# Spreading attention weights over key bands on 128 partitions instead of 80, with 64x32 matmul tiles and a new order of instructions

## The chip, the cores and the metric

The kernel runs on one core of a Trainium2 chip. A core has five engines that run at the same time, each with its own queue of instructions: PE (TensorE: matmuls and transposes against an identity), DVE (VectorE), ACT (ScalarE), POOL (GpSimd) and SP (SyncE, which here only issues DMAs). Engines wait for each other through semaphores. The metric is the time of one execution on the device in microseconds (us). Three executions of the kernel before took 189.2, 189.23 and 190.11 us, a median of 189.23. The profiled execution is a separate one, with a time of its own.

## The reference

The input is 2048 rows of 448 numbers. One attention layer and one MLP layer with a shift between rows follow each other, each behind a layernorm and with a residual:

```python
qkv = x @ wqkv                                # 16 heads of 28, S = 2048 rows
idx = pos[:, None] - 2 * arange(8)[None, :]   # 8 keys per query, every second row back
logits = einsum("bhsd,bhswd->bhsw", q, k[idx]) * 28 ** -0.5   # -1e9 where idx < 0
attn = softmax(logits)
A = einsum("bhsw,bhswd->bhsd", attn, v[idx]) @ wo

h  = gelu(layernorm(y) @ w1)
hs = concat(four quarters of h, shifted by +1, -1, +2, -2 rows) @ w2
x1 = y + hs
B  = x1 + gelu(layernorm(x1) @ w3) @ w4

y   = x + A(layernorm(x))
out = y + B(y)
```

w1 and w2 are 448 x 448, w3 is 448 x 1792 and w4 is 1792 x 448.

## The kernel before, in words

The rows are taken in four blocks of 512 (t = 0 to 3), each of four tiles of 128 rows. Per block the stages are N1 (layernorm, and the turning of its result so that the features lie on partitions), A1 (q and k), V (v), A2 (the logits: DVE multiplies q by shifted k, the products `qk_r`, and PE sums them over a head's features), S (softmax and the turning of its result), A3 (the weighted sum over v), O (w_o and the residual), B1 (layernorm) and M (w1 and gelu). The rest goes by five units of tiles (u = 0 to 4): B2 (w2 on shifted columns), T (layernorm), W3 (w3 and gelu) and B3 (w4, the residual and the store).

The change touches the way from the softmax to the weighted sum. A query needs eight keys that lie two rows apart. `phase_A2` ends with a multiplication that writes the normalised weights p into `pb`: for each of 8 groups of 64 queries, a row of 80 keys (16 of them, `PADK`, belong to the group before), of which each query fills its eight. PE turns `pb` against the identity in 64-row halves, so that keys lie on partitions, and copies put it into `pt[t]` (80 x 1024). `phase_A3` goes four times per block (`il`) over 128 queries. DVE multiplies a slice of `pt` with the 0/1 mask `bmask` (80 x 64), spread out so that every query has its own column: `bd_r` (80 x 2048). This is the group "bd_r<-arena,bmask" of the profile. PE then does 32 matmuls, with weights from `vw` (v, 80 keys by 32 columns for one head) and 64 moving columns of `bd_r`, on four column tiles of the array (j), into one PSUM bank, and one copy takes the bank to `actT`, the input of O. `vw` is v with its keys moved to the right partitions: `phase_V` copies v into `vt` (128 rows a tile) and issues DMAs from `vt` to `vw`: `a` (64 rows), `b` (80 rows) and `c` (the 16 rows of padding of three tiles) for each block, and `p` (the padding from the block before) from block 1 on.

Other transfers on SP are the loads of the inputs and weights, small copies within "arena" that give k its padding and its last 64 features their second half (the "kk" and "kr" pieces), the stores, and the DMA transposes `actT<-lntm`, which turn a normalised block where the table `TURN` says `d`.

The order of all instructions is written out by hand in the list `ORDER`: each number is one recorded operation (an instruction or a group of matmuls), and each engine gets its own operations in this order. `OTHER` lists the operations that go to their second engine: PSUM copies by default run on ACT and then on DVE, and the p multiplication by default on DVE and then on POOL. The tables `NORM`, `STATS` and `POWER` choose engines for the layernorms' parts. `arrange` (L191) adds the rule on transposes: a DMA transpose waits for all plain DMAs (stores aside) issued since the transpose before it, and all plain DMAs after it wait for it. All recorded instructions are issued by one line, L983, so that a line number tells nothing in this profile, and the names of the tiles and their shapes do.

PE, DVE, ACT and SP therefore each work through a fixed queue. An instruction whose input is late holds up all that stand behind it on its engine.

Of the kernel before, what the change touches and what calls it, by code (L numbers as in the profile page):

```python
# [6 lines left out]
ALU = mybir.AluOpType  # L7
# [10 lines left out]
RESIDUAL = 'ttvv'  # L18
ORDER = """
# [29 lines left out]
"""  # L49
OTHER = """  # L50
102 186 187 381 490 493 496 499 502 505 549
# [229 lines left out]
def bass_sequential_preLN__sliding_local_dilated__mixer_s_mlp__prompt_kernel(  # L281
# [9 lines left out]
    PADK = 16  # L291
    KW = 80
    KVW = PADK + 512
# [17 lines left out]
    with ExitStack() as es:  # L311
# [5 lines left out]
        bd_r = sb("bd_r", [KW, NBD, 2048], BF16)  # L317
        vt = sb("vt", [128, 2, 4, 512], BF16)
        vw = sb("vw", [KW, 2, 8, 512], BF16)
        bmask = sb("bmask", [KW, 64], BF16)  # L320
        lntm = sb("lntm", [128, NLN, 4, 512], BF16)
        actT = sb("actT", [128, NACT, 4, 4, 128], BF16)
        h3T = sb("h3T", [128, NF + 2, 512], BF16)
        wo_s = sb("wo_s", [128, 4, D], BF16)
# [92 lines left out]
        for z in (vt[:].rearrange("p s i (h n) -> p (s i h) n", n=32)[:, :, DH:32], pb[:], wo_s[:]):  # L417
            dve("memset", ap=z, constant=0.0)
# [606 lines left out]
```

## Time and profile before

| what | before |
| --- | --- |
| median of 3 runs (lowest, highest) | 189.23 us (189.2, 190.11) |
| profiled execution: its time, its span | 189.32 us, 187.5 us |
| PE busy, matmuls | 179.2 us (96% of the span), 2434 |
| DVE busy, instructions | 126.6 us (68%), 224 |
| ACT busy, instructions | 123.9 us (66%), 282 |
| POOL busy | 29.2 us (16%) |
| granted PE clock | 0.999 |
| DMA | 18.06 MB, 96 GB/s on average |

The span is the time from the first to the last recorded instruction, and the run's own time is 1.82 us longer than it. A busy share is an average over the whole span; the stretches differ much. In the slices, each digit is the busy share of one fortieth of the span in tenths. A group row reads: line, engine, operation, output and inputs with their shapes, count, then busy us in total and mean ns of one, then the idle time just before these instructions and what ended it. The mean length of one matmul or copy is longer than its pitch where instructions of one engine overlap. In a row of the chain of waits stand the start, the length and the work that the end depends on, in order of time. A row of a timeline gives the start, the length up to the last end, the instructions and their count.

### The profile page before, as it was taken

What the parts mean: (1) busy time and instruction counts of PE and PEld (TensorE: products, weight loads), DVE (VectorE), ACT (ScalarE), POOL (GpSimd) and SP (SyncE); (2) the same over time, 40 slices, a digit from 0 to 9 for tenths busy, and PEclk for the clock granted to TensorE, in tenths of its full rate; (3) what the DMA queues carried; (4) which work ended last, traced back from release to release, by engine and by line L of the source; (5) the groups of instructions that cost most, each with busy time, mean ns of one, the idle gap of its engine ahead of it and who ended that gap; (6) DMA issues with size and microseconds to landing.
All of it is one profiled execution on the core that took longest, in us unless ns stands there. A gap on an engine that the chain in (4) does not pass through costs nothing.

```text
span 187.5 us, 5641 instructions
## 1 busy us (share of the span) xinstructions
PE 179.2 (96%) x2434; PEld 102.4 (55%) x2434; DVE 126.6 (68%) x224; ACT 123.9 (66%) x282; POOL 29.2 (16%) x63
## 2 busy tenths in 40 slices
PE   6999999999988799999999999999999999999994
PEld 2694434355443345477445555555556665666882
DVE  7799999999999999997297278470057357000503
ACT  4679999989999897988976447505775004822340
POOL 4230000000004101004801200200002662500000
PEclk9999999999999999999999999999999999999999
DMA  5995724676644655453645000371000432400111
GB/s 133 359 286 100 105 59 101 112 177 128 144 129 75 155 144 139 121 154 104 117 126 98 3 0 3 68 149 36 0 0 3 89 96 77 105 3 0 66 36 49
DMA packets 36577, 18.06 MB, mean 96 GB/s; under 512 B 25304, under 2 KB 36040, under 8 KB 36552
## 3 DMA queue, kind: packets, MB, share of 16 engines
q1 hardware_dynamic: 36552, 17.70, 40.2%
q8 instruction: 19, 0.31, 0.7%
q14 instruction: 6, 0.05, 0.1%
HBM read 7.91 MB, written 1.84 MB: 52 GB/s over the span
## 4 chain that ended last, share of the span: by engine, by line
PE 78%; ACT 12%; DVE 4%; DMA 4%; issue 1%; SPq 0%
PE ps L983 78%; ACT arena L983 5%; ACT lntm L983 3%; DMA actT<-lntm 2%; ACT vt L983 2%; DVE st L983 1%; DMA xin<-in_A_x_dram 1%; ACT xin L983 1%; DVE lntm L983 1%; DVE bd_r L983 1%; DVE qk_r L983 1%; ACT rs_x L983 0%; DVE ls L983 0%; DVE mx L983 0%; DVE mv L983 0%
## 5 line engine op out<-in xcount | busy, mean ns | idle before, releaser
L983 PE MATMUL ps<-actT,arena 64*128 64x512 bf16 (+1 forms) x756 | 69.1, 329 | 0.4 <-ACT vt L983 0.4
L983 ACT ACTIVATE h3T<-ps 128x512 bf16<-128x512 f32 (+1 forms) x70 | 31.1, 515 | 40.8 <-PE ps L983 40.5
L983 PEld LDWEIGHTS ps<-actT,arena 64*128 64x128 bf16 x756 | 38.8, 94 | 24.9 <-PE ps L983 0.8
L983 PE MATMUL ps<-arena,h3T 64*128 64x448 bf16 (+2 forms) x434 | 43.7, 343 | 0.1
L983 ACT ACTIVATE arena<-ps 128x512 bf16<-128x512 f32 (+3 forms) x62 | 31.3, 544 | 7.0 <-PE ps L983 6.4
L983 PEld LDWEIGHTS ps<-arena,h3T 64*128 64x128 bf16 (+1 forms) x434 | 26.3, 94 | 16.1 <-PE ps L983 0.5
L983 DVE TENSOR_TENSOR qk_r<-arena 128x4096 bf16<-128x4096 bf16 (+1 forms) x16 | 32.0, 2014 | 0.0
L983 DVE SCALAR_TENSOR_TENSOR qk_r<-ps,mrs,arena 128x448 bf16<-128x448 f32 (+1 forms) x17 | 10.5, 652 | 30.9 <-PE ps L983 25.4
L983 POOL TENSOR_TENSOR arena<-arena,xin 128x448 f32<-128x448 f32 x16 | 16.1, 1037 | 19.8 <-DVE lntm L983 19.8
L983 DVE TENSOR_TENSOR bd_r<-arena,bmask 80x2048 bf16<-80x2048 bf16 x16 | 18.8, 1210 | 0.0
L983 DVE SCALAR_TENSOR_TENSOR arena<-xin,rs_y,ps 128x448 f32<-128x448 bf16 x16 | 10.2, 674 | 11.6 <-PE ps L983 9.6
L983 PE MATMUL ps<-wo_s,actT 64*128 64x448 bf16 x128 | 14.4, 350 | 1.0 <-ACT actT L983 0.7
L983 PE MATMUL ps<-w_s,arena 64*128 64x448 bf16 (+1 forms) x128 | 14.2, 350 | 0.4 <-ACT arena L983 0.3
L983 PE MATMUL ps<-actT,w_s 64*112 64x512 bf16 x112 | 13.4, 379 | 0.8 <-DMA actT<-lntm 0.6
L983 PE MATMUL ps<-arena,actT 64*128 64x448 bf16 x112 | 12.4, 350 | 0.1
L983 ACT ACTIVATE lntm<-xin,nm 128x448 bf16<-128x448 bf16 x16 | 10.5, 663 | 2.4 <-DVE nm L983 2.4
L983 POOL TENSOR_TENSOR pb<-ls,mx 128x512 bf16<-128x512 f32 x2 | 3.5, 1730 | 48.3 <-ACT mx L983 48.3
L983 ACT ACTIVATE actT<-ps 128x512 bf16<-128x512 f32 (+2 forms) x18 | 10.6, 645 | 0.0
L983 PEld LDWEIGHTS ps<-actT,w_s 64*112 64x112 bf16 x112 | 7.1, 127 | 6.3 <-PE ps L983 1.0
L983 PEld LDWEIGHTS ps<-wo_s,actT 64*128 64x128 bf16 x128 | 5.8, 94 | 7.6 <-ACT actT L983 1.9
L983 PEld LDWEIGHTS ps<-w_s,arena 64*128 64x128 bf16 (+1 forms) x128 | 6.4, 94 | 6.6 <-PE ps L983 1.0
L983 DVE BATCH_NORM_STATS2 st<-xin 128x6 f32<-128x448 bf16 x16 | 9.1, 614 | 0.9 <-DMA xin<-in_A_x_dram 0.9
(71 smaller groups left out, 160.9 us busy)
## 6 DMA issues: line engine op xcount, KB each, us to landing
arena<-in_B_w_dram SPq DMA_DIRECT2D x2, 896.0 KB, 5.5
out_dram<-qk_r SPq DMA_DIRECT2D x15, 112.0 KB, 1.8
arena<-in_B_w_dram SPq DMA_DIRECT2D x2, 784.0 KB, 5.0
vw<-vt SPq DMA_DIRECT2D x4, 320.0 KB, 3.2
vw<-vt SPq DMA_DIRECT2D x4, 256.0 KB, 4.7
arena<-in_A_wqkv_dram SPq DMA_DIRECT2D x2, 448.0 KB, 4.5
xin<-in_A_x_dram SPq DMA_DIRECT2D x2, 448.0 KB, 6.9
xin<-in_A_x_dram SPq DMA_DIRECT2D x3, 224.0 KB, 5.2
```

The source lines that it names most:

```text
L983: inst = getattr(eng, meth)(**kw)
```

## The change

The table `BAND` gives each block a form: blocks 0 to 2 take the new one ("h"), block 3 the old one ("w"). In the new form, bands of 32 queries by 48 keys stand on both halves of the partitions (rows 0 to 47 and 64 to 111). The p multiplication writes `pb_h` (128 columns a group instead of 80), PE turns 64x128 pieces of it, and `pt` has 128 rows. A3 goes twice over a pair of tiles (256 queries): one DVE multiplication of 128 x 2048 with a mask `bmask_h` (128 x 32), then two groups of 64 matmuls with 48x32 weights and 32 moving columns, on eight tiles of 64x32 (two row halves by four column tiles), into two banks, one for each half, and a copy for each bank. The matmuls of the kernel go from 2434 to 2818.

The DMAs that fill `vw` are cut otherwise in blocks 0 to 2: four pieces (32, 48, 48 and 48 rows) instead of two (64 and 80 rows), and `c` and `p` as before: two more DMAs a block. The setup has one more memset on DVE (`pb_h`), a memset and two mask selections on POOL and two reductions on DVE (`bmask_h`).

`ORDER` and `OTHER` are new throughout. Among other things, ACT has 10 table loads instead of 12 and two normalisations fewer, DVE has two normalisations more and two copies of 128x512 fewer (and one of 64x256 more); between the DMA transposes of blocks 2 and 3 stand ten plain DMAs instead of six, and between that of block 3 and the first of B1 18 instead of 16. `V_FIRST` is False and changes nothing.

```diff
...
 RESIDUAL = 'ttvv'
+BAND = 'hhhw'
+V_FIRST = False
 ORDER = """
-8 9 10 12 13 29 7 0 1 39 40 41 42 43 30 44 33 14 15 16 17 18 19 20 21 22 23 45 46 47 6 34 5 35 2 48 32 50 51 36 55 56
...
+9 10 11 8 5 13 14 15 16 17 18 19 20 21 22 23 0 1 3 4 45 46 47 6 48 49 50 30 31 39 40 2 7 56 51 52 53 54 41 57 61 62 58
...
 OTHER = """
-102 186 187 381 490 493 496 499 502 505 549
+192 193 195 282 355 389 496 499 505 511 555 556
...
+    QB, KB = 32, 48
...
-        bd_r = sb("bd_r", [KW, NBD, 2048], BF16)
+        bd_r = sb("bd_r", [128, NBD, 2048], BF16)
         vt = sb("vt", [128, 2, 4, 512], BF16)
-        vw = sb("vw", [KW, 2, 8, 512], BF16)
+        vw = sb("vw", [128, 2, 8, 512], BF16)
         bmask = sb("bmask", [KW, 64], BF16)
+        bmask_h = sb("bmask_h", [128, QB], BF16)
...
+        pb_h = sb("pb_h", [128, NSM, NW * 128], BF16)
...
-        pt = [arv(A_KV + t * KVB + 4 * KVW, KW, 1024) for t in range(NST)]
+        pt = [arv(A_KV + t * KVB + 4 * KVW, KW if BAND[t] == "w" else 128, 1024) for t in range(NST)]
...
-        for z in (vt[:].rearrange("p s i (h n) -> p (s i h) n", n=32)[:, :, DH:32], pb[:], wo_s[:]):
+        for z in (vt[:].rearrange("p s i (h n) -> p (s i h) n", n=32)[:, :, DH:32], pb[:], pb_h[:], wo_s[:]):
...
+            par = ls[:, 0, 168:192].bitcast(BF16).rearrange("p (e j) -> p e j", e=2)
+            pool("memset", ap=par, constant=0.0)
+            for base in (0, 64):
+                pool("affine_select", out=par, in_=par, pattern=[[1, 2], [2, KB // 2]], compare_op=ALU.not_equal, fill=1.0, base=base, channel_multiplier=-1)
+            for e in range(2):
+                dve("tensor_reduce", out=bmask_h[:].rearrange("p (m e r) -> p m e r", m=2, e=2)[:, :, e, :],
+                    in_=bass.AP(par.tensor, par.offset + e * (KB // 2) + 1, [list(par.ap[0]), [8, 2], [1, NW], [1, 8]]), axis=AX.X, op=ALU.max)
...
-            dma("vwa%d" % sl, vw[PADK:KW, sl, 0:8:2, :], vt[0:64, sl, :, :], 64 * 4096)
-            dma("vwb%d" % sl, vw[0:KW, sl, 1:8:2, :], vt[48:128, sl, :, :], 80 * 4096)
+            if BAND[t] == "w":
+                pieces = (("a", PADK, 0, 0, 64), ("b", 0, 1, 48, 128))
+            else:
+                pieces = (("a", PADK, 0, 0, QB), ("b", 64, 0, PADK, 64), ("d", 0, 1, 64 - PADK, 64 + QB), ("e", 64, 1, 64 + PADK, 128))
+            for name, to, odd, lo, hi in pieces:
+                dma("vw%s%d" % (name, sl), vw[to:to + hi - lo, sl, odd:8:2, :], vt[lo:hi, sl, :, :], (hi - lo) * 4096)
             dma("vwc%d" % sl, vw[0:PADK, sl, 2:8:2, :], vt[112:128, sl, 0:3, :], 16 * 3072)
...
             row = lambda v, off, step: bass.AP(v, off, [[v.shape[1] * v.shape[2], 128], [step, NW], [16, 4], [DIL, NW], [1, DIL]])
-            mult = dict(out=row(pb, sl * NW * KW + DIL, KW + DIL), in0=row(ls, sl * 512, 64),
-                        in1=bass.AP(zs, sl * 64, [[64 * NSM, 128], [8, NW], [2, 4], [0, NW], [1, DIL]]), op=ALU.mult)
+            by_half = lambda v, off, step, half: bass.AP(v, off, [[v.shape[1] * v.shape[2], 128], [step, NW], [half, 2], [16, 2], [DIL, NW], [1, DIL]])
+            whole = BAND[t] == "w"
+            if not whole:
+                mult = dict(out=by_half(pb_h, sl * NW * 128 + DIL, 128 + DIL, 64), in0=by_half(ls, sl * 512, 64, QB),
+                            in1=bass.AP(zs, sl * 64, [[64 * NSM, 128], [8, NW], [4, 2], [2, 2], [0, NW], [1, DIL]]), op=ALU.mult)
+            else:
+                mult = dict(out=row(pb, sl * NW * KW + DIL, KW + DIL), in0=row(ls, sl * 512, 64),
+                            in1=bass.AP(zs, sl * 64, [[64 * NSM, 128], [8, NW], [2, 4], [0, NW], [1, DIL]]), op=ALU.mult)
             S.add("dve", "tensor_tensor", alts=[("pool", [("tensor_tensor", mult)])], **mult)
             banks = [_Tile(P_bank), _Tile(P_bank)]
 
             def turn(h, r):
                 part = (TOP, BOT)[h]
-                return (h, dict(out=banks[h](lambda v: v[0:KW, 64 * r:64 * r + 64]), lhsT=pb[part, sl, r * KW:(r + 1) * KW], rhs=ident[part, part],
-                                start=True, stop=True), 64)
+                src = pb[part, sl, r * KW:(r + 1) * KW] if whole else pb_h[part, sl, r * 128:(r + 1) * 128]
+                return (h, dict(out=banks[h](lambda v: v[0:src.shape[1], 64 * r:64 * r + 64]), lhsT=src, rhs=ident[part, part], start=True, stop=True), 64)
 
             steps([turn(h, r) for r in range(NW) for h in range(2)])
             for h, b in enumerate(banks):
-                copy(pt[t].rearrange("p (n r) -> p n r", r=NW)[:, 64 * h:64 * h + 64, :], b(lambda v: v[0:KW, :].rearrange("p (r n) -> p n r", r=NW)))
+                copy(pt[t].rearrange("p (n r) -> p n r", r=NW)[:, 64 * h:64 * h + 64, :], b(lambda v: v[0:KW if whole else 128, :].rearrange("p (r n) -> p n r", r=NW)))
 
         def phase_A3(t):
             a = _Tile(P_act)
             sl = t % 2
-            for il in range(4):
+            for il in range(4 if BAND[t] == "w" else 0):
                 bd = _Tile(P_bd)
                 b = _Tile(P_bank)
-                dve("tensor_tensor", block=True, out=bd(lambda v: v.rearrange("p (n g r) -> p n g r", g=8, r=NW)),
+                dve("tensor_tensor", block=True, out=bd(lambda v: v[0:KW, :].rearrange("p (n g r) -> p n g r", g=8, r=NW)),
                     in0=pt[t][:, il * 256:il * 256 + 256].rearrange("p (n r) -> p n r", r=NW).unsqueeze(2).broadcast_to([KW, 32, 8, NW]),
                     in1=bmask[:].rearrange("p (g r) -> p g r", r=NW).unsqueeze(1).broadcast_to([KW, 32, 8, NW]), op=ALU.mult)
                 mms([(b(lambda v, j=j, lo=128 * c + 64 * a2: v[32 * j:32 * j + 32, lo:lo + 64]),
-                      vw[:, sl, 2 * il + a2, (4 * c + j) * 32:(4 * c + j) * 32 + 32],
-                      bd(lambda v, lo=(16 * a2 + 4 * c + j) * 64: v[:, lo:lo + 64]), True, True, 64, j)
+                      vw[0:KW, sl, 2 * il + a2, (4 * c + j) * 32:(4 * c + j) * 32 + 32],
+                      bd(lambda v, lo=(16 * a2 + 4 * c + j) * 64: v[0:KW, lo:lo + 64]), True, True, 64, j)
                      for c in range(4) for a2 in range(2) for j in range(4)])
                 copy(a(lambda v, il=il: v[:, il, :, :].rearrange("p c n -> p (c n)").rearrange("p (m r e) -> p m r e", r=NW, e=2)),
                      b(lambda v: v.rearrange("p (m e r) -> p m r e", r=NW, e=2)))
+            for pair in range(2 if BAND[t] == "h" else 0):
+                bd = _Tile(P_bd)
+                banks = [_Tile(P_bank), _Tile(P_bank)]
+                dve("tensor_tensor", block=True, out=bd(lambda v: v.rearrange("p (n g r) -> p n g r", g=4, r=NW)),
+                    in0=pt[t][:, pair * 512:pair * 512 + 512].rearrange("p (n r) -> p n r", r=NW).unsqueeze(2).broadcast_to([128, 64, 4, NW]),
+                    in1=bmask_h[:].rearrange("p (g r) -> p g r", r=NW).unsqueeze(1).broadcast_to([128, 64, 4, NW]), op=ALU.mult)
+                for il in range(2):
+                    specs = []
+                    for c in range(4):
+                        for a2 in range(2):
+                            for half in range(2):
+                                for j in range(4):
+                                    keys = slice(64 * half, 64 * half + KB)
+                                    at = (il * 8 + 2 * c + a2) * QB
+                                    specs.append((("matmul", dict(out=banks[half](lambda v, j=j, at=at: v[32 * j:32 * j + 32, at:at + QB]),
+                                                                  lhsT=vw[keys, sl, 4 * pair + 2 * il + a2, (4 * c + j) * 32:(4 * c + j) * 32 + 32],
+                                                                  rhs=bd(lambda v, keys=keys, lo=(16 * (2 * il + a2) + 4 * c + j) * QB: v[keys, lo:lo + QB]),
+                                                                  start=True, stop=True)), (QB, "q", 4 * half + j)))
+                    S.group("pe", [x for x, _ in specs], pe=[y for _, y in specs])
+                for half, b in enumerate(banks):
+                    copy(a(lambda v, lo=2 * pair, half=half: v[:, lo:lo + 2, :, :].rearrange("p i c (u h m r e) -> p (i c u) h m r e", u=2, h=2, m=2, e=2)[:, :, half, :, :, :]),
+                         b(lambda v: v.rearrange("p (u m e r) -> p u m r e", u=16, m=2, e=2)))
```

More of the change, by code (lines that the diff above doesn't have):

```diff
@@ L435, in bass_sequential_preLN__sliding_local_dilated__mixer_s_mlp__prompt_kernel @@
         act(zs[:, 0, 0:1], epsilon[:, 0:1], ACT.Exp)
+        if V_FIRST:
+            load_rows("wv", wqkv_s[:, :, 2 * D:3 * D], A_wqkv, 2 * D, D)
         load_rows("wqk", wqkv_s[:, :, 0:2 * D], A_wqkv, 0, 2 * D)
@@ L438, in bass_sequential_preLN__sliding_local_dilated__mixer_s_mlp__prompt_kernel @@
         load_x(6, 2)
-        load_rows("wv", wqkv_s[:, :, 2 * D:3 * D], A_wqkv, 2 * D, D)
+        if not V_FIRST:
+            load_rows("wv", wqkv_s[:, :, 2 * D:3 * D], A_wqkv, 2 * D, D)
         for i in range(8, NTL, 4):
```

56 rows, old and new, of the table ORDER are left out of this document.

## The prediction

> **What bounds the kernel now.** I read the page's slices and chain first, then busy time by stretches of the span, then the chain near its one gap, and last the rows of the engines that feed that gap. In the slices, TensorE (PE) is nearly full from end to end, and VectorE (DVE) and ScalarE (ACT) are full only up to the middle:
>
> ```profile
> PE   6999999999988799999999999999999999999994
> ...
> DVE  7799999999999999997297278470057357000503
> ACT  4679999989999897988976447505775004822340
> ...
> PE 78%; ACT 12%; DVE 4%; DMA 4%; issue 1%; SPq 0%
> ```
>
> Busy time by stretches (start:end, length, then PE, weight loads, DVE, ACT, POOL, clock, DMA share, GB/s):
>
> ```profile
> 20.00:36.00 16.00, 15.57 (x193) 6.99 (x189) 16.00 (x17) 15.69 (x42) 0.00 (x0) 1.00 0.64 111
> 36.00:48.00 12.00, 12.00 (x242) 5.99 (x240) 11.82 (x12) 10.60 (x27) 0.00 (x0) 1.00 0.58 120
> 48.00:63.00 15.00, 12.41 (x270) 6.03 (x266) 14.88 (x23) 14.52 (x38) 2.47 (x3) 1.00 0.53 121
> 63.00:82.00 19.00, 18.44 (x306) 8.92 (x302) 18.51 (x31) 17.32 (x31) 1.01 (x1) 1.00 0.52 135
> ```
>
> DVE has no spare time from 20 to 82 us, ACT next to none, and PE lacks work only in 48:63 (2.59 us idle). The chain of waits shows what ended that idle time:
>
> ```profile
> 53.94 0.48 ACT actT L983
> ...
> 56.23 1.12 DVE bd_r L983
> 57.36 0.34 DVE lntm L983
> ...
> 58.04 4.52 DMA actT<-lntm
> 62.60 1.09 PE ps L983 x8
> ...
> 66.42 1.09 ACT arena L983 x2
> ...
> 89.52 94.75 PE ps L983 x1103
> ```
>
> ACT's last piece and DVE's normalisation finish block 0's layernorm, the DMA transpose carries it, and at 62.60 the w1 matmuls of block 0 ("M0") start. From there PE is almost unbroken to the end. So the time is the start of M0 plus 121.7 us of PE (to 184.27) and the last tiles' exit, and what is before M0 counts only as far as it brings that start forward.
>
> **The change, part by part.** *The spreading on DVE.* These rows group DVE's instructions between 10 and 82 us (count, then busy us and mean ns):
>
> ```profile
> L983 DVE TENSOR_TENSOR qk_r<-arena 128x4096 bf16<-128x4096 bf16 x12 | 27.3, 2281 | 0.0
> L983 DVE TENSOR_TENSOR bd_r<-arena,bmask 80x2048 bf16<-80x2048 bf16 x12 | 14.2, 1211 | 0.0
> ...
> L983 DVE TENSOR_TENSOR qk_r<-arena 128x2048 bf16<-128x2048 bf16 x4 | 4.9, 1214 | 0.0
> ```
>
> Blocks 0 to 2 go from twelve 80x2048 multiplications to six of 128x2048. A product of 128x2048 takes 1214 ns against 1211 for 80x2048, so partitions cost nothing and each instruction keeps its price: 6 x 1.21 = 7.3 us of DVE goes. Added or moved on to DVE, from the whole span's groups:
>
> ```profile
> L983 DVE TENSOR_SCALAR lntm<-xin,nm,rs_y 128x512 bf16<-128x512 bf16 x14 | 5.2, 416 | 0.0
> ...
> L983 DVE CAST actT<-ps 128x512 bf16<-128x512 f32 x4 | 2.6, 686 | 1.0 <-PE ps L983 0.9
> ...
> L983 DVE TENSOR_REDUCE bmask<-ls 80x32 bf16<-80x256 bf16 x2 | 0.8, 383 | 0.0
> ...
> L983 DVE TENSOR_SCALAR lntm<-arena,nm,rs_y 128x512 bf16<-128x512 f32 x1 | 0.5, 543 | 0.0
> ...
> L983 DVE MEMSET pb<- 128x320 uint32 x1 | 0.3, 325 | 0.0
> ```
>
> A memset 512 wide (325 x 512/320 = 0.52 us); two reductions for the new mask, at most as long as the old pair (0.77 us; half as many outputs, so I take 0.5); and two normalisations taken over from ACT (0.42 + 0.54). Two PSUM copies of 0.69 us go back to ACT and one of half the columns comes instead (I take 0.4): -1.0. Sum on DVE: -7.3 + 0.5 + 0.5 + 1.0 - 1.0 = about -6.3 us, nearly all before 82 us. ACT loses two normalisations of 0.81 us (its 128x512 form with the bias) and takes two copies of 0.48 (the chain's piece at 53.94), -0.7 in all; its table loads drop from 12 to 10:
>
> ```profile
> L983 ACT ACT_TABLE_LOAD x6 | 7.7, 1283 | 0.1
> ...
> L983 ACT ACTIVATE lntm<-xin,nmr,rs_y 128x512 bf16<-128x512 bf16 x2 | 1.6, 809 | 0.0
> ```
>
> That is up to 2.6 us more of ACT. On POOL one memset and two mask selections come at setup, beside other work: nothing on the path.
>
> *How much of DVE's relief reaches M0.* The listing of the new order puts DVE's layernorm for M0 some 2.8 us earlier in DVE's own queue than before (57.70 becomes 54.9), and ACT's 54.4 becomes about 53. Late next is SyncE's (SP) DMA queue, where each transpose waits for every plain DMA since the one before it, and later ones wait for the transpose:
>
> ```profile
> 25.00 1.32 SPq L983 DMA_DIRECT2D vw<-vt  x2
> 26.36 1.53 SPq L983 DMA_DIRECT2D arena<-arena  x2
> 27.93 1.31 SPq L983 DMA_DIRECT2D vw<-vt  x2
> 31.80 2.91 SPq L983 DMA_TRANSPOSE actT<-lntm  x1
> 36.45 0.65 SPq L983 DMA_DIRECT2D arena<-arena  x1
> ...
> 47.52 0.61 SPq L983 DMA_DIRECT2D arena<-in_B_w_dram  x1
> 48.18 0.64 SPq L983 DMA_DIRECT2D vw<-vt  x1
> 58.04 2.89 SPq L983 DMA_TRANSPOSE actT<-lntm  x1
> ```
>
> Each of blocks 0 to 2 gets two more loads of vw. The new order has ten plain DMAs ahead of block 3's transpose instead of six. Six took 25.00 to 29.24, 0.71 us each, so four more cost up to 2.8 us; some of that was waiting, so I take 2.3: the transpose is issued at 34.1 and, 4.6 us later as before, the queue goes on at 38.8. Before M0's transpose it then issues 18 instead of 16. The 16 took 36.45 to 48.82, or 0.77 each; 18 take 13.9 and end at 52.7. What they take from issue to landing:
>
> ```profile
> arena<-in_B_w_dram SPq DMA_DIRECT2D x2, 896.0 KB, 5.5
> ...
> vw<-vt SPq DMA_DIRECT2D x4, 320.0 KB, 3.2
> vw<-vt SPq DMA_DIRECT2D x4, 256.0 KB, 4.7
> ...
> arena<-arena SPq DMA_DIRECT2D x3, 12.0 KB, 1.9
> ```
>
> The load of w3 (issued at 47.52 before) is now fourteenth of the 18, so issued at 48.8 and landed at 54.3; the last vw piece, issued at 51.9, lands after 3.2 to 4.7, at 55.1 to 56.6, of which I take the middle, 55.8. Before, the last issue ended 9 us ahead of the transpose; now the queue sets the time. M0's transpose goes from 58.04 to about 55.8: -2.2 us. The floor is PE itself: its idle time in 48:63 is 2.59, so M0 cannot move by more than about 2.6 for the same work ahead of it.
>
> One copy of k's padding (12 KB) moves behind M0's transpose, as second: issued at about 61.0, landed at 62.9. Its reader, a product of block 3, stands 7.7 us behind M0's normalisation in DVE's queue, at about 62.6; DVE waits 0.3 us there, and PE has M0's own 28 matmuls to do meanwhile (3.8 us, by 1.09 for eight): nothing on the path.
>
> *PE.* The spread matmuls as one group, and then two stretches of them on PE's timeline (start, us to the last end):
>
> ```profile
> L983 PE MATMUL ps<-bd_r,vw 80*32 80x64 bf16 x512 | 5.9, 195 | 0.4 <-DVE bd_r L983 0.3
> ```
>
> ```profile
> 54.52 0.42 PE L983 MATMUL ps<-bd_r,vw 80*32 80x64 bf16 x32 [0.31 <-DVE bd_r L983]
> ...
> 66.30 0.99 PE L983 MATMUL ps<-bd_r,vw 80*32 80x64 bf16 x96
> ```
>
> 96 take 0.99 and 32 take 0.42, so 32 more matmuls cost 0.285 us, 8.9 ns each. Now twelve times 32 matmuls on four column tiles become twelve times 64 on eight tiles with half the columns. If columns set the pace, eight at a time over 32 columns take half: -0.14 x 12 = -1.7 us. If each instruction costs its 8.9 ns, it is +0.285 x 12 = +3.4. I take 0, the middle: half the columns in as many rounds. [...]
>
> Turning pb goes through 128-column instead of 80-column weights, 48 pairs, within 0.2 us either way. The order has 28 changes between tile shapes instead of 33; at some 0.1 us, the gap that the rows above leave after taking 0.285 from 0.42 (0.13), that is -0.5, of which about -0.2 lies behind M0. By the listing, PE has the same work queued from M0 on, within 0.1 us, and only block 2's four spread groups are in it.
>
> Sum: -2.2 (M0) - 0.2 (shapes) = -2.4 on a span of 187.5, so 185.1; the profiled execution took 189.32, 1.82 more than its span and 0.09 over the median of 189.23. Forecast 186.9 us.
>
> **The rivals.** *All of the relief passes.* The DMA queue keeps its old pace of 0.65 per issue, M0 comes at its floor (-2.6), ACT's 1.09 at 66.42 goes, since DVE runs some 6 us ahead by then, all the shape changes count (-0.5), and the columns halve in block 2 (4 x 0.14 = 0.6): 187.5 - 4.8 + 1.8 = 184.5. For it: DVE idles nowhere up to 82. Against: the same stretch has ACT nearly as full.
>
> *PE pays per instruction.* +0.285 x 8 = 2.3 us ahead of M0 fill the 2.59 of idle time, M0 starts at about 62.3, and block 2 adds 1.1 behind it: 187.5 - 0.3 + 1.1 - 0.2 + 1.8 = 189.9, no change. For it: 64 weight loads and 64 matmuls per group are to be issued instead of 32. Against: the four column tiles already overlap, 195 ns of mean length at one per 8.9 ns. The change not doing what it says is this case too: halves that run one after the other.
>
> *The DMA queue makes it slower.* Six more transfers pass through a queue in which a transpose waits for all of them. If a piece of vw waits for its data, or two of the pieces' landings stretch, 18 issues at 1.1 instead of 0.77 end at 38.8 + 19.8 = 58.6, and the last lands 3 later, at 61.6: M0's transpose is 3.5 late, 187.5 + 3.5 - 0.2 + 1.8 = 192.6; at 0.95 it is about 190. It decides as soon as the last landing passes 58.04, that is at a mean pitch above 0.9. For it: a piece of 256 KB takes longer to land (4.7) than one of 320 (3.2), so time goes by what else is in flight, and more pieces need not add bytes to add time. Against: the pieces carry the same bytes in all. [...]
>
> **How the numbers follow.** Forecast as summed (185.6 to 188.2): 0.42. All passes (about 184.3 to 185.6): 0.20. PE per instruction, or ACT holding the pace: 0.14, no change. DMA queue, alone or with PE's price on top, over 190.2: 0.24. So faster 0.62, same 0.14, slower 0.24, where within 0.5% (0.95 us) is about what a measurement can tell from no change (the three runs spread over 0.9). The range takes in the first three and the nearer half of the last: 184.3 to 191.0; the forecast's own is 185.6 to 188.2.
>
> **What would show it.** Right: six spreads of 128x2048 at 1.21 us; M0 at about 60.4, its transpose released by the last vw piece or w3, not by DVE; groups of 64 matmuls at about 0.4 us; PE unbroken after. Wrong: M0 after 62, groups of 64 at 0.7 us, or new idle time of PE behind M0, where block 1's transpose or that of the next unit comes late. The largest doubt is the pace of the DMA queue between the two transposes.

## The result, and the profile after

The changed kernel is slower: 202.75 us (201.06 to 204.63) against 189.52 (189.2 to 190.11), a ratio of 1.0665 (95% interval 1.059 to 1.074). The ratios here and below compare undisturbed executions alone, and the medians are of all. The profiled execution took 201.06 us with a span of 199.3, 11.8 more than before. Its page, first the slices and the chain:

```profile
PE   6999999696979995999999999999999999999994
...
DVE  7879999998275788598749316876006786000402
ACT  4589998944697595697797585127683003650340
...
PEclk9999999996996997899999999999999999999999
...
PE 75%; ACT 12%; issue 4%; DMA 4%; DVE 3%; SPq 1%
```

PE now has three notches between 44 and 80 us (a six, a seven and a five), and at the same places or in the slice behind the granted clock drops, which it never did in the profiled execution before (40 nines in that line, a mean of 0.999). (The six just ahead of them, at 35 to 40 us, is a wait of 1.55 us for a DMA transpose.) DVE has become idle in the same stretch. In the chain "issue", time in which an engine waited for nothing that the profile shows, has grown from 1% to 4%. The same stretches as before (start:end, length, PE, weight loads, DVE, ACT, POOL, clock, DMA share, GB/s):

```profile
36.00:48.00 12.00, 8.23 (x340) 5.24 (x338) 11.04 (x11) 6.98 (x19) 0.00 (x0) 0.95 0.68 134
48.00:63.00 15.00, 12.95 (x364) 7.43 (x366) 7.96 (x11) 12.33 (x32) 0.00 (x0) 0.84 0.47 119
63.00:82.00 19.00, 16.24 (x394) 9.00 (x390) 13.73 (x21) 13.46 (x28) 1.36 (x1) 0.89 0.55 98
```

PE's timeline shows what the notches are (start, length to the last end, the matmuls and their count, in brackets the idle time before them and what ended it):

```profile
43.01 1.46 PE L1030 MATMUL ps<-bd_r,vw 48*32 48x32 bf16 x139
46.70 1.29 PE L1030 MATMUL ps<-bd_r,vw 48*32 48x32 bf16 x117 [2.22 <-issue]
47.91 1.46 PE L1030 MATMUL ps<-actT,arena 64*128 64x512 bf16 x6
49.17 1.21 PE L1030 MATMUL ps<-wo_s,actT 64*128 64x448 bf16 x5
50.70 0.55 PE L1030 MATMUL ps<-wo_s,actT 64*128 64x448 bf16 x3 [0.32 <-issue]
...
60.21 0.86 PE L1030 MATMUL ps<-bd_r,vw 48*32 48x32 bf16 x84 [1.73 <-issue]
...
77.52 0.87 PE L1030 MATMUL ps<-bd_r,vw 48*32 48x32 bf16 x82 [2.48 <-issue]
```

Each stall cuts through the middle of a row of the new matmuls: 139 run, PE stands still for 2.22 us, 117 more run. No semaphore ends the wait. Between the stall that ends at 46.70 and the next one, which ends at 50.70, lie 117 + 6 + 5 = 128 matmuls, and each has a weight load, so 256 instructions. The clock around the first stall, in steps of 2 us:

```profile
44.00:46.00 2.00, 0.48 (x39) 0.34 (x27) 1.19 (x3) 1.36 (x4) 0.00 (x0) 1.00 0.41 53
46.00:48.00 2.00, 1.30 (x119) 1.22 (x121) 2.00 (x1) 0.00 (x0) 0.00 (x0) 0.68 0.67 136
48.00:50.00 2.00, 2.00 (x11) 0.63 (x11) 1.25 (x2) 1.72 (x4) 0.00 (x0) 0.50 0.32 75
50.00:52.00 2.00, 1.68 (x17) 0.70 (x16) 0.00 (x0) 0.84 (x2) 0.00 (x0) 0.96 0.72 143
```

Behind the stall PE runs at half its clock (0.50) for 3.41 us, from 46.73; the two other stretches of half clock, from 60.38 and from 77.45, are as long. As groups over the whole span (count, busy us, mean ns, idle before them):

```profile
L1030 PE MATMUL ps<-bd_r,vw 48*32 48x32 bf16 x768 | 7.9, 187 | 6.7 <-issue 6.4 <-ACT arena L1030 0.3
L1030 DVE TENSOR_TENSOR bd_r<-arena,bmask_h 128x2048 bf16<-128x2048 bf16 x6 | 7.2, 1222 | 4.5 <-ACT arena L1030 4.5
```

The spreads on DVE did go from twelve to six at the forecast price (1222 ns). But 6.4 us of PE's idle time stands in front of the new matmuls, and the mean clock of 0.974 over 199.3 us is another 5.2 us of lost work. Together that is 11.6 us, about as much as the 11.8 by which the span grew; what DVE saved and what the extra DMAs cost then have to cancel, which is not shown here.

### The profile page after: what moved, and what is told of

Same layout as the page of the kernel before. It is cut to its first block, busy times and chain, and to the rows that moved or that the text cites. A ratio compares the mean times of both kernels' runs of the same rounds, so it can differ in the third digit from the quotient of the medians.

```text
span 199.3 us, 6414 instructions
## 1 busy us (share of the span) xinstructions
PE 185.4 (93%) x2818; PEld 102.8 (52%) x2818; DVE 123.3 (62%) x222; ACT 120.8 (61%) x279; POOL 27.8 (14%) x66
## 4 chain that ended last, share of the span: by engine, by line
PE 75%; ACT 12%; issue 4%; DMA 4%; DVE 3%; SPq 1%
PE ps L1030 75%; ACT arena L1030 5%; ACT lntm L1030 2%; DMA actT<-lntm 2%; DMA arena<-arena 1%; DVE st L1030 1%; ACT actT L1030 1%; ACT h3T L1030 1%; ACT vt L1030 1%; ACT L1030 1%; DVE qk_r L1030 1%; SPq L1030 1%; ACT rs_x L1030 1%; ACT rs_y L1030 0%; DVE wo_s L1030 0%
## 5 line engine op out<-in xcount | busy, mean ns | idle before, releaser
L1030 PE MATMUL ps<-actT,arena 64*128 64x512 bf16 (+1 forms) x756 | 70.0, 333 | 1.9 <-DMA actT<-lntm 1.6
L1030 PEld LDWEIGHTS ps<-actT,arena 64*128 64x128 bf16 x756 | 37.4, 95 | 30.5 <-ACT actT L1030 1.7
L1030 PE MATMUL ps<-arena,h3T 64*128 64x448 bf16 (+2 forms) x434 | 45.0, 343 | 0.3 <-ACT h3T L1030 0.3
L1030 PEld LDWEIGHTS ps<-arena,h3T 64*128 64x128 bf16 (+1 forms) x434 | 24.0, 94 | 18.5 <-ACT h3T L1030 0.9
L1030 PE MATMUL ps<-wo_s,actT 64*128 64x448 bf16 x128 | 16.1, 367 | 0.3 <-issue 0.3
L1030 PE MATMUL ps<-bd_r,vw 48*32 48x32 bf16 (+1 forms) x896 | 9.2, 188 | 6.7 <-issue 6.4
L1030 ACT ACTIVATE actT<-ps 128x512 bf16<-128x512 f32 (+2 forms) x19 | 11.3, 642 | 5.3 <-PE ps L1030 5.3
L1030 PEld LDWEIGHTS ps<-bd_r,vw 48*32 48x32 bf16 (+1 forms) x896 | 8.2, 92 | 9.2 <-issue 8.3
L1030 PEld LDWEIGHTS ps<-wo_s,actT 64*128 64x128 bf16 x128 | 7.3, 100 | 7.4 <-issue 3.0
L1030 DVE TENSOR_TENSOR bd_r<-arena,bmask_h 128x2048 bf16<-128x2048 bf16 x6 | 7.2, 1222 | 4.5 <-ACT arena L1030 4.5
```

What stands on the lines that cost most here:

```text
L1030: inst = getattr(eng, meth)(**kw)
```

## The experiments

Two theories stood against each other. F, an estimate from the rows above: PE's instructions arrive in pieces of 256 (the 128 matmuls and weight loads between two stalls), a piece takes about 4 us to arrive (4.00 from 46.70 to 50.70), and a piece that PE uses up faster leaves it waiting; 128 of the new matmuls in a row are such a piece. T: the tiles of 64x32, or the new order, make PE wait by themselves.

**Half the matmuls, the same tiles.** Of the changed kernel's inner loop:

```diff
-                        for a2 in range(2):
-                            for half in range(2):
-                                ... 32 columns of key tile a2, weights of key tile a2
+                        for half in range(2):
+                            ... 2 x 32 columns of both key tiles, weights of the first
```

> The changed kernel, but each group of 64 spread matmuls becomes 32: one matmul takes the 32 columns of both key tiles at once (64 columns), with the first tile's v for both, so the second tile's v is left out of the sum; tiles, banks, DMAs, DVE work and order stay. Theory F (PE's instructions are fetched in pieces of 256, and a piece used up in under about 4 us leaves PE waiting): the four stalls of PE in the spread groups (2.2, 0.8, 1.7 and 2.5 us) go, the clock stays at 1.0, and the time falls from 202.7 to 187 to 190 us. Rival T (row-half tiles or the order make PE wait): the stalls stay at over 1 us each, and the time stays above 198.

190.9 us (190.33 to 192.42), 1.0052 of before (1.0018 to 1.0085), mean clock 1.000 in nine of ten executions. The group row of the spread matmuls:

```profile
L1029 PE MATMUL ps<-bd_r,vw 48*32 48x64 bf16 x384 | 4.2, 195 | 0.2 <-ACT arena L1029 0.2
```

Of 6.4 us in issue nothing is left ahead of them (0.34 and 0.45 us stand at two other places, both within w_o's matmuls), and 11.9 us of the 13.2 that the change cost are gone. Tiles, banks, DMAs and order are those of the changed kernel, so these are not what stalls PE. That it is not faster than before (I had expected 187 to 190) is a second question (below).

**Twice the matmuls in the kernel before.**

```diff
-                      bd(lambda v, lo=(16 * a2 + 4 * c + j) * 64: v[:, lo:lo + 64]), True, True, 64, j)
-                     for c in range(4) for a2 in range(2) for j in range(4)])
+                      bd(lambda v, lo=(16 * a2 + 4 * c + j) * 64 + m * h: v[:, lo:lo + m]), True, True, m, j)
+                     for c in range(4) for a2 in range(2) for h in range(parts) for j in range(4)])
```

Here `parts` is 2 and `m` 32 in blocks 0 to 2, and 1 and 64 in block 3.

> The kernel before, with each spread matmul of blocks 0 to 2 cut into two of 32 columns on the same 80x32 tile and weights: 2818 matmuls as in the changed kernel, nothing else changed. Theory F: stretches of more than about 128 matmuls at 8 ns appear in it (64, 128 and 192 in a row where 32, 64 and 96 stood), so stalls of 1 to 2.5 us in issue appear on PE and the clock falls behind them; time 193 to 200. Rival T: no stall of PE over 0.6 us that is put down to issue; only the matmuls' own price, 0.25 x 12 = 3 us at most, so 189 to 192.5.

197.88 us (196.35 to 199.51), 1.0408 (1.0358 to 1.0457). PE's timeline behind M0 (the stall in block 0 is 1.83 us):

```profile
68.67 3.77 PE L985 MATMUL ps<-actT,w_s 64*112 64x512 bf16 x28 [1.22 <-DMA actT<-lntm]
72.37 1.62 PE L985 MATMUL ps<-bd_r,vw 80*32 80x32 bf16 x173
76.16 0.30 PE L985 MATMUL ps<-bd_r,vw 80*32 80x32 bf16 x19 [2.17 <-issue]
```

The old tiles, the old DMAs and the old order, and only the number of matmuls doubled, give the same stall, and the time lies in the range of F. T falls for the tiles.

**The order alone, and the form alone.** For the first, `BAND` is 'wwww' in the changed kernel, and each operation keeps its counterpart's place. For the second, the changed kernel's code takes the list `ORDER` of before, each new operation at the place of its old counterpart.

```diff
-BAND = 'hhhw'
+BAND = 'wwww'
```

> The changed kernel with the old form in all blocks (80x32 tiles, two vw pieces a block, four spreads on DVE), in the new order: each old operation stands where its counterpart of the new form stood. The setup for the new mask stays. Theory F: no stalls in issue, clock 1.0; DVE has its 7.3 us back, so 189 to 195, late by what the order expects of DVE. Rival O (the new order is itself the cause): 198 or more, with PE idle before block 3's second stage and block 0's w1 as in the changed kernel.

> The new form in blocks 0 to 2 in the old order: each new operation stands where its old counterpart stood, the two copies of a pair after both groups. Theory F: groups of 64 stand 1, 2 and 3 in a row, so PE stalls in issue where over 128 matmuls of 8 ns fall into one piece of 256 instructions; one to three stalls of 1 to 2.5 us, time 190 to 199. Rival O: no stalls, 186 to 189.

The order alone: 196.3 us (195.84 to 198.19), 1.037 (1.0315 to 1.0425). It has no stall in issue; instead PE waits for DVE, which has its twelve spreads back (PE's group row of that kernel):

```profile
L1030 PE MATMUL ps<-bd_r,vw 80*32 80x64 bf16 x512 | 6.1, 194 | 4.3 <-DVE bd_r L1030 4.0 <-DMA vw<-vt 0.3
```

I had expected a clock of 1.0 here, and that was wrong: its mean is 0.982, with two stretches of half clock behind waits for DVE and ACT of 1.30 us and less. Of the second, in steps of 2 us:

```profile
70.00:72.00 2.00, 0.50 (x41) 0.30 (x32) 2.00 (x3) 2.00 (x5) 0.00 (x0) 1.00 0.45 62
72.00:74.00 2.00, 1.48 (x42) 0.92 (x44) 2.00 (x2) 1.67 (x5) 0.00 (x0) 0.85 1.08 133
74.00:76.00 2.00, 2.00 (x14) 0.78 (x11) 2.00 (x2) 1.97 (x4) 0.00 (x0) 0.50 0.34 75
```

So the order fits the new form only; by itself it costs 6.6 us, of another kind, and I had put the upper edge of that too low by 1.3. The form alone: 202.36 us (202.08 to 204.06), 1.0689 (1.064 to 1.0738), as slow as the whole change, with stalls of 1.88 and 2.37 us in issue. It came out above my range of 190 to 199: I counted the stalls and left out the clock, which was at half in three stretches, two of them behind the stalls and one (from 63.02) behind a wait of 1.03 us for DVE.

**One block, and the same block with its groups apart.** Block 2 alone has the new form, in the order of before; then the same instructions, with PE's order behind M0 changed: the list shows the operations on PE (394, 395, 399 and 400 are the four groups of 64).

```diff
-... 399 394 395 545 403 400 546 404 407 483 485 320 316
+... 394 545 395 546 403 404 399 483 485 320 316 400 407
```

> The new form in block 2 alone, in the order before (the setup for both masks, four vw pieces in block 2). Its four groups of 64 stand almost together behind M0, so one piece of 256 PE instructions holds nothing but spread matmuls (1.05 us). Theory F: exactly one stall of PE put down to issue, 2.2 to 2.8 us, there, and one or two windows of half clock behind it: 193 to 196. Rival T: no such stall, 189.5 to 191.5.

> The kernel of the run above, block 2 alone in the new form, with the same instructions; only the order of PE behind M0 differs: between the four groups of 64 stand those of w2, w_o, block 3's sums and block 1's w1, so that by the durations of the traces every piece of 256 instructions there lasts 3.3 us or more. Theory F: the stall is under 0.8 us or gone, and the time 1.5 to 4.5 us below that run, 189.5 to 192.5. Rival T (the tiles stall by themselves): idle time in issue as in that run, 193 or more.

195.18 us (194.49 to 195.61), 1.0258 (1.021 to 1.0307), and apart 194.35 (193.63 to 194.76), 1.0214 (1.0158 to 1.027). PE's timeline, first together:

```profile
67.12 1.62 PE L1030 MATMUL ps<-bd_r,vw 48*32 48x32 bf16 x173
71.02 0.26 PE L1030 MATMUL ps<-bd_r,vw 48*32 48x32 bf16 x19 [2.29 <-issue]
...
74.31 0.67 PE L1030 MATMUL ps<-bd_r,vw 48*32 48x32 bf16 x64
```

and apart:

```profile
67.95 0.65 PE L1030 MATMUL ps<-bd_r,vw 48*32 48x32 bf16 x64
69.20 0.93 PE L1030 MATMUL ps<-w_s,arena 64*128 64x448 bf16 x8 [0.60 <-ACT arena L1030]
70.06 0.65 PE L1030 MATMUL ps<-bd_r,vw 48*32 48x32 bf16 x64
...
77.23 0.66 PE L1030 MATMUL ps<-bd_r,vw 48*32 48x32 bf16 x64
79.12 0.93 PE L1030 MATMUL ps<-wo_s,actT 64*128 64x448 bf16 x8 [1.23 <-ACT actT L1030]
```

One piece full of short matmuls makes exactly one stall, 2.29 us, and the mean clock falls to 0.991. Apart, the stall behind M0 is gone and the clock is 1.000, with the same 256 matmuls on the same tiles. The time fell by only 0.8, where I expected 1.5 or more. M0 itself starts 0.83 us later (64.25 against 63.42), and a stall of 0.50 in issue now stands ahead of it, in a group of the old form (58.90). Behind M0, w_o and w2 now wait for ACT (1.23, 0.60 and 0.37), so waits of the order stand where the wait in issue stood. That this stall goes with the spacing is shown, a gain from it is not.

These rows give the price of a matmul, too: 173 take 1.62 us and 64 take 0.65, so 109 more cost 0.97, or 8.9 ns each, as much as the old ones with twice the columns on half the tiles. (On the eight tiles with 64 columns, in the half-matmul kernel, 128 take 1.38 and 64 take 0.70, or 10.6 ns each.)

A cruder attempt put groups off all over the changed kernel:

> The changed kernel with all its work; only the order differs: the groups of 64 spread matmuls are put off until, by the durations of the traces, any 256 PE instructions (128 matmuls and their weight loads) around them last 3.6 us or more, and what depends on them is put off with them. Theory F: no stall in issue over 0.8 us, clock 1.0, 189.5 to 194. Rival T (the 64x32 tiles stall wherever they stand): the idle time put down to issue in the spread groups stays at 5 us or more and the time above 198.

258.42 us (255.29 to 263.44), 1.3456. PE's group row of the spread matmuls:

```profile
L1030 PE MATMUL ps<-bd_r,vw 48*32 48x32 bf16 x768 | 8.0, 185 | 1.2 <-ACT arena L1030 1.2
```

Idle time in issue, 6.4 us ahead of these 768 matmuls in the changed kernel, is gone here, where T wanted 5 or more. But w_o, the loads of vw and the transposes behind them were put off as well: M0 starts at about 82, 12 us later than in the changed kernel. As a time this run says nothing, and my forecast for it missed by more than 60 us.

**Where the stalls stand in PE's queue.** The traces can settle F directly. Number PE's recorded instructions (matmuls, weight loads and the few of its sequencer) from 0. The four stalls of 0.3 us or more that are put to issue in the changed kernel stand at 1217, 1473, 1985 and 2753, each 193 more than a multiple of 256. Counted by their matmuls, to within one instruction, seven stalls of other kernels, old form and new, stand at such numbers as well: 1473 and 2753 with twice the old matmuls and with the form alone, 2241 with the new form in block 2, 1217 with half the matmuls and 1729 with four vw pieces (below). And each of the changed kernel's four ended after a packet of 16 KB of the instruction queue had landed: the packets landed at 45.20, 49.38, 58.81 and 76.11, and PE went on at 46.69, 50.70, 60.21 and 77.52, 1.3 to 1.5 us later. Counting blocks and packets from the start, it is each time the block's own packet. No other block starts sooner after its packet either: the shortest distance is 1.3 us in the changed kernel and 2.7 in the one before.

The short matmuls are not the only way to such a stall, though. In the kernel before with four vw pieces (below), which has no new matmul, the profiled execution shows one:

```profile
59.74 0.32 PE L987 MATMUL ps<-bd_r,vw 80*32 80x64 bf16 x18 [1.33 <-issue]
```

PE had taken 5.1 us over the block ahead of it, but the packet came late: it began 4.1 us after that block was entered, where the packets ahead of the changed kernel's four stalls began after 0.8 to 1.1. What held it back is not known. And in the changed kernel a block entered at 116.82 is followed by the next at 119.03, after 2.2 us, without a stall: that one's packet had landed at 117.07. So in these traces the stall goes by whether the next packet has come.

**What one stall costs.** A wait of known length in the kernel before:

```diff
+        hold = pool("memset", ap=bd_r[:, 0, :], constant=0.0)
+        hold.deps.add(S.ops[717])
+        S.ops[725].deps.add(hold)
```

> The kernel before; in the stretch of matmuls of the last third, one group of w4 waits for a POOL memset that starts when the group ahead of it is done, so that PE stands still once for about 2.3 to 2.6 us. Theory C (the clock that follows a stall costs as much again): granted clock near 0.5 for about 3.4 us behind it, 1.7 us more, 193.2 to 194.4 in all. Rival: only the idle time, clock 1.0, 191.7 to 192.5.

192.87 us (191.41 to 195.04), 1.0198 (1.0125 to 1.0271). PE's row in the profiled execution:

```profile
148.25 3.96 PE L987 MATMUL ps<-arena,h3T 64*128 64x448 bf16 x40 [2.26 <-POOL bd_r L987]
```

In that execution the clock stayed at 1.000 and the time was 191.41; another had 1.000 and 192.57, and the other two a mean clock of 0.991 and 193.17 and 195.04. So a single stall of 2.3 us need not be followed by half clock. That the lower clock of the other two came from the stall is not shown: they have no trace, and of 23 executions of the kernel before, without the wait, three have a mean of 0.990 or 0.991 as well (191.22 to 191.43 us). Each of my expectations fits some of the executions, so neither is borne out. More telling are the four executions of the kernel with twice the old matmuls: their mean clocks are 0.983, 0.991, 0.983 and 1.000, so the same program had two such stretches, one or none. A mean lower by 0.009 over some 191 us is 1.7 us, just what 3.4 us at half clock would cost, and the means of the changed kernel's four runs (0.974, 0.966, 0.966, 0.958) are three to five such steps.

**The DMA queue.** Two runs: the four vw pieces alone in the kernel before, and the half-matmul kernel with two pieces.

```diff
-            dma("vwa%d" % sl, vw[PADK:KW, sl, 0:8:2, :], vt[0:64, sl, :, :], 64 * 4096)
-            dma("vwb%d" % sl, vw[0:KW, sl, 1:8:2, :], vt[48:128, sl, :, :], 80 * 4096)
+            pieces = (("a", PADK, 0, 0, 32), ("b", 48, 0, 32, 64), ("d", 0, 1, 48, 96), ("e", 48, 1, 96, 128))
```

> The kernel before with each block's two large vw pieces cut into four in blocks 0 to 2 (rows 32, 32, 48, 32), the second of each right behind the first; nothing else. Theory D (the queue of DMAs holds up block 0's transpose): block 3's transpose is issued 1.3 to 2.8 us later, block 0's B1 transpose at 58.5 to 60 instead of 58.04, 190.2 to 191.5. Rival (hidden): that transpose stays at 58.0 to 58.3 and the time within 0.5% of before.

```diff
-                pieces = (("a", PADK, 0, 0, QB), ("b", 64, 0, PADK, 64), ("d", 0, 1, 64 - PADK, 64 + QB), ("e", 64, 1, 64 + PADK, 128))
+                pieces = (("a", PADK, 0, 0, 96), ("b", 0, 1, 48, 128))
```

> The changed kernel with 32 instead of 64 spread matmuls in a group, as in the first of the runs above (the second key tile's v left out of the sum), and now with two vw pieces of 96 and 80 rows a block instead of four, the same bytes in two transfers fewer; order as changed. If the number of transfers is what holds block 0's B1 transpose at 59.2 in that run: it is issued at 56.5 to 58, M0 starts at 61 to 62.5, and the time is 188 to 189.8. If not: 59 or later and 190.3 to 191.3 as there.

The pieces alone: 191.99 us (189.91 to 195.4), a ratio of 1.0049 (1.0001 to 1.0098), about 0.9 us. In the profiled execution, one of 195.4 us, block 3's transpose was issued at 33.08, 1.28 later than before, and block 0's at 58.79. But there the last vw piece had landed at 57.95 and DVE's normalisation ended at 58.37, so DVE held that transpose, not the queue. Nor is the 0.9 the price of the transfers alone: six of the ten executions have a mean clock of 0.991 or less, and the four at 1.000 took 189.91 to 190.35 us. Two transfers fewer a block: 189.21 us (188.37 to 190.95), 0.9958 (0.9926 to 0.9989). The transposes of block 3 and of M0 on SP, with four pieces and half the matmuls:

```profile
34.91 1.74 SPq L1029 DMA_TRANSPOSE actT<-lntm  x1
...
52.37 1.28 SPq L1029 DMA_DIRECT2D vw<-vt  x2
59.23 1.80 SPq L1029 DMA_TRANSPOSE actT<-lntm  x1
```

and with two:

```profile
32.84 1.84 SPq L1029 DMA_TRANSPOSE actT<-lntm  x1
...
56.93 3.05 SPq L1029 DMA_TRANSPOSE actT<-lntm  x1
```

Both transposes come 2.1 to 2.3 us earlier, as expected, and the kernel gains 1.7 us (190.9 to 189.21) and passes below the kernel before. Of the 2.3 us at M0's transpose, the queue itself gave 1.2: with four pieces the last one landed at 59.22, when DVE's normalisation had ended at 57.77, and with two pieces DVE holds the transpose again, to 56.66. With the stalls and the extra transfers out of the way, the rest of the change is worth 0.8 us (0.2 to 1.4). That kernel leaves out part of the sum and is no version to use.

**M0 earlier without the change.** In the kernel before, DVE's order only:

```diff
-375 186 376 271 288 272 467 189 377 276 364 366 187
+186 187 189 375 376 271 288 272 467 377 276 364 366
```

(186, 187 and 189 are normalisations of block 0's B1, 189 moved from ACT; 375 and 376 belong to block 2's softmax.)

> The kernel before; on DVE the normalisations of block 0's B1 come directly behind their scale, ahead of block 2's maximum, difference and block 1's last spread, and one of ACT's two normalisations goes to DVE as well. If DVE's order is what holds M0 before: its transpose at about 56 instead of 58.04, M0 at 60.3 to 60.8, 187.0 to 188.3. If the DMA queue or PE's own work stands right behind it: M0 at 62 or later, 188.8 to 189.8.

190.76 us (190.0 to 193.68), 1.0047 (1.0007 to 1.0086). The transpose was issued at 56.12, as aimed. PE's rows ahead of M0 in the kernel before, and then in this one:

```profile
61.47 0.49 PE L983 MATMUL ps<-ident,pb 64*80 64x64 bf16 x16 [0.59 <-POOL arena L983]
62.60 1.77 PE L983 MATMUL ps<-actT,w_s 64*112 64x512 bf16 x11 [0.65 <-DMA actT<-lntm]
```

```profile
62.12 0.49 PE L983 MATMUL ps<-ident,pb 64*80 64x64 bf16 x16 [0.28 <-POOL arena L983]
62.45 3.75 PE L983 MATMUL ps<-actT,w_s 64*112 64x512 bf16 x28
```

In PE's queue the turning of block 2's p stands ahead of M0 and waits for POOL. It is done only about 0.65 us before M0 can start in the kernel before. A transpose two us earlier therefore brings M0 forward by 0.15 us here, because block 2's softmax went back for it. M0 stayed where the second of my expectations had it, but the time is above both ranges. No version that computes the whole sum beat the kernel before.

## Why the prediction was wrong

**The step that failed is PE's term.** "I take 0, the middle" was wrong twice. A matmul with half the columns on twice the tiles costs the same 8.9 ns, so the per-instruction end of my own bounds (+3.4 us for twelve groups) was right. And the larger part was in no rival: the stalls in issue (6.4 us) and the half clock (5.2 us). I priced "PE pays per instruction" at 189.9, since I took PE to be able to issue at 8.9 ns for as long as it likes. The rows that I priced from show 96 such matmuls in a row (192 instructions); that their price holds over 512 in a row was the assumption that I did not state. The kernel before has a longer row, in block 3, which does not stall:

```profile
100.99 1.29 PE L983 MATMUL ps<-bd_r,vw 80*32 80x64 bf16 x128
```

It lies across the edge of two blocks (the second is entered at 101.29 and lasts 4.9 us). The row of 256 matmuls in block 0 of the changed kernel is long enough to hold a whole block.

The traces hold one more trace of it, the instruction queue (packets, MB, share of the DMA engines), before and after:

```profile
q8 instruction: 19, 0.31, 0.7%
```

```profile
q8 instruction: 22, 0.36, 0.9%
```

A packet is some 16 KB. The changed kernel has 384 matmuls and so 768 instructions more, and three packets more: 256 instructions each, which agrees with the 128 matmuls and 128 weight loads between two stalls. PE stood still where it had used up a block before the next packet had come: the stalls that end at 46.70 and 50.70 are 4.0 us apart with one block between them, and 128 matmuls at 8.9 ns last 1.1 us.

The half clock is likewise no part of the forecast. In the changed kernel three stretches of it, 3.41 us each, came at the end of stalls of 2.22, 1.73 and 2.48 us (the stall of 0.32 us had none of its own); in the order-alone kernel they came behind several waits of 1.30 us and less. The idle time of 2.59 us in 48:63 of the kernel before, split into waits under 0.8 us each, was not enough: the clock there is 1.00. The idle time alone does not decide: in the form-alone kernel PE was busy for 2.38 of the 3.41 us ahead of the stretch from 63.02, and in the order-alone kernel for 1.65 of the 3.41 us from 56.34, where the clock stayed at 1.00. What does is open.

**DVE: right in price, wrong in what it brings.** Six spreads cost 1222 ns each, the memset 0.49 us (0.52 forecast), two reductions 0.54 (0.5). But the listing was to bring DVE's normalisation for M0 some 2.8 us forward, from 57.70 to 54.9. In the half-matmul kernel, without the large stalls, DVE waits for ACT on the way, and the normalisation ends at 57.77:

```profile
51.05 0.17 DVE L1029 TENSOR_SCALAR nm<-mv 128x4 f32<-128x4 f32 x1 [1.36 <-ACT xin L1029]
...
57.37 0.40 DVE L1029 TENSOR_SCALAR lntm<-xin,nm,rs_y 128x512 bf16<-128x512 bf16 x1
```

So DVE's relief did not reach M0; with two vw pieces 1.0 us of it did (56.66).

**The DMA queue: right in kind, too small.** I took block 3's transpose at 34.1 and M0's at 55.8. Without the stalls they came at 34.91 and 59.23. The pitch of the 18 issues was near the forecast (39.24 to 53.65, 0.80 each); what failed is the last landing: the last piece, issued at about 53.0 (the second of the two in the row at 52.37), held the transpose until 59.23, 6.2 us, where I took 3.2 to 4.7. The rival "the DMA queue makes it slower" named the point where it decides (58.04), and it was passed, by 1.2 us instead of 3.5. By the run with two pieces the extra transfers cost 1.7 us there. In the changed kernel itself the queue was not what held M0: its last piece landed at 58.75, and SP's wait ahead of the transpose at 64.58 is one for DVE's normalisation, which came late behind the stalls (engine, line, what it waited for, us in total, times, longest):

```profile
SPq L1028 <- DVE lntm L1030: 9.0, 1, 9.0
```

**M0's floor: wrong.** I gave PE's idle time of 2.59 us as the floor. The row at 61.47 shows a nearer one: block 2's turning, which waits for POOL, stands ahead of M0 in the same queue, and its own wait is 0.59 us. With both gates, an earlier transpose alone is worth at most the 0.65 us that M0 waits behind it. I read which wait ended last and not which would end next.

**"The same work from M0 on": wrong.** From M0 (69.93) to the end of PE's work it took 126.2 us instead of 121.7; the stall of 2.48 us, the clock and block 2's groups lie in it.

## What to carry to other kernels

Before many short instructions take the place of a few, count them in a row on their engine: the price of 8.9 ns, taken from a short burst, did not hold here where a block of 256 was used up before the next 256 had arrived; at the changed kernel's stalls the next block started 3.6 to 4.1 us after the one before. Such a stall showed as idle time in "issue" that cuts a group of equal instructions in two (2.22 us between 139 and 117 matmuls), with no semaphore behind it, and the clock that dropped behind such stalls cost nearly as much again (5.2 us beside 6.4). And when a wait is to be shortened, read the wait that stands next to it in the same queue first: that, and not the idle time of the stretch, is the most that can be won (0.65 us here, not 2.59).

## What the runs showed of the hardware that I had not expected

A matmul of 48 rows by 32 columns on eight tiles cost 8.9 ns in a stream, the same as one of 80 rows by 64 columns on four tiles. In the changed kernel PE stopped for 1.7 to 2.5 us three times, where it had used up a block of 256 of its instructions in 1.4 to 2.0 us and the packet with the next had not come, and it went on 1.3 to 1.5 us after that packet had landed. Kernels with old and new tiles had the stall at the same distance (173 matmuls behind M0 in both). The clock fell to half in three stretches of 3.41 us, each 1.7 us of lost time, and the kernel with twice the old matmuls has none, one or two such steps in different executions (mean clock 1.000, 0.991 and 0.983). Two transfers fewer a block, with the same bytes, brought block 3's transpose forward by 2.1 us.
